# Attention and FFN in one kernel: the main heads begin beside the last early pairs, and fewer FFN pieces stand beside the first of them

## The chip, the cores and the metric

The kernel runs on one core of a Trainium2 chip. The core has five engines with an instruction queue each, and every queue is worked in order: TensorE (PE in the profile, its weight loads PEld), VectorE (DVE), ScalarE (ACT), GpSimd (POOL) and SyncE (SP), which here only issues DMAs. The metric is the device time of one execution in microseconds (us); lower is better.

## What is computed

Attention with a forget gate over 8 batches of 8 heads, 576 positions, head size 64, all in float32, and behind it a feed-forward network (FFN) over the 4608 rows of 512 that the attention leaves:

```
scores = scale * q @ k.T
cum    = cumsum(log(clip(f, 1e-4, 1)))
scores = where(causal, -1e9, scores + cum[:, None] - cum[None, :])
attn   = exp(scores - max); attn = attn / (sum + 1e-9)
x      = (attn @ v), heads side by side: 4608 x 512
h      = x @ w_in                 # 512 -> 2048
out    = max(0.01 * h, h) @ w_out # 2048 -> 512
```

## The kernel before

**Precision.** A float32 matmul is done as products of split numbers: each operand is a high part, rounded to the type float32r, and a low part (what the rounding left). Names that end in h and l (xh and xl, win_h and win_l, gh and gl, ph and pl) are such parts. For q and k the parts lie in the two halves of the 128 partitions: s1 and m1 hold high and low parts of one head's q and k, s2 and m2 (tiles fixed_s2a, fixed_m2b and so on, a and b by turns) the same crosswise, with the decay in spare rows.

**Two kinds of attention work.** The first 256 positions of three batches (NE = 3) are done ahead, two heads at a time, as 12 *early pairs* (functions early_load, early_scores, early_values; tiles qk, ve, ze, sce, tre, pte, ave, xe). This makes rows for the FFN soon, while its weights still come in: they are 16 pieces of a megabyte that load_weight fetches into two buffers (wraw) and splits on ACT and DVE. Then come the 64 *main heads*, t = 0 to 63, in the order of batches 0, 3 to 7, 1, 2. In batches 0, 1 and 2 a main head has 320 rows left (three row tiles, i = 2 to 4), in the others all 576 (five row tiles).

**A main head** passes through these steps. load(t) issues the DMAs of q and k into raw (one buffer) and of v into vm (one buffer). split(t) casts raw to s1 and m1 on ACT (L362, L363), copies parts of it to the other 64 partitions by DMA, and subtracts on POOL (minus, L149: m2 first, then s1) to get the low parts; v goes to fixed_vs, cast on ACT (L373), subtracted and shifted on POOL. scores(t, i) makes the row tile's scores on PE (sc), adds the mask and takes the row maximum on DVE (L395, into fixed_z0 to fixed_z4) and the exponential on ACT (L401); for the last tile POOL copies a corner of z4 (L407). In the next pass of the loop transposes(t, i) turns the tiles on PE (tr) and evacuates them on ACT (ph, L445) and DVE (pl, L447). values(t) multiplies with V (av) and adds the halves into x. After each second head, inverse and normalise make 1 / sum: its rows go by SP's queue to DRAM and come back spread over partitions (rows, rb and ph in the DMA lists).

**The FFN** takes 18 groups of 256 rows. It is a generator, ffn(), that yields after each *quantum*: 12 matmuls into h (half of a piece of 256 hidden units) or 6 into o (128 output rows). A piece p of a group is 4 quanta. Groups 0 and 1 are done in halves, pieces 0 to 3 of both and then 4 to 7 of both, since the weights come in that order; what the first halves leave is kept in the tiles part. The low part gl of the activation is made on POOL (L617) while heads run and on DVE else. Groups from 2 on are read back from DRAM (xs) and split by split_group: a cast on DVE (xh) and a subtraction of 128 x 1024 on POOL (xs, L149).

**What sets the order.** fill(n) adds n to a credit and takes as many whole quanta as it covers. Beside the early pairs the table FQ gives the credit of each step. In the loop over main heads a pass calls fill nine times' worth of step, and step is min(have / (left + SLACK), MAXQ) / 8: quanta at hand, divided by the passes left until new rows come, plus a reserve. The program so written is then listed for each engine by a scheduler, which may move instructions over one another where no dependence forbids it; tc.keep_in_program_order holds a single one in its place. So the order on each engine is that of the built program, not quite that of the text.

**Tiles that share buffers.** Tiles with one tag use the same buffer in turn. The fixed tiles of the main heads (fixed_z, vm, s2, m2, vs) are cleared once by fix(), on POOL. Before, the early pairs used the tags vm, s2b, m2b, s2a and m2a for half of their tiles (ZE and L316), so those fixed tiles could not be made until the pairs were done.

## Time and profile before

| | |
|---|---|
| median of three runs | 1210.83 us (1210.63, 1210.83, 1215.83) |
| the profiled execution | 1211.98 us, span 1210.2 |
| busy: PE, DVE, ACT, POOL | 98%, 52%, 53%, 38% |
| DMA | 110.55 MB, mean 91 GB/s |
| end of the early pairs (last ave), first score of head 0 | 145.5 us, 157.9 us |

The span is cut into 40 slices of 30 us on the page; each digit is the busy share of an engine in tenths, and PEclk the clock that the throttle granted to TensorE:

```profile
PE   9999989999999999999999999999999999999998
POOL 0000255555555444454444353534454544531000
PEclk9999999999999999999999999999999999999999
```

Matmuls are pipelined: one lasts longer in the trace than the distance to the next, so a PE that reads as busy all the time can still lose a little at every short wait.

### The profile page before, as it was taken

What the parts mean: (1) busy time and instruction counts of PE and PEld (TensorE: products, weight loads), DVE (VectorE), ACT (ScalarE), POOL (GpSimd) and SP (SyncE); (2) the same over time, 40 slices, a digit from 0 to 9 for tenths busy, and PEclk for the clock granted to TensorE, in tenths of its full rate; (3) what the DMA queues carried; (4) which work ended last, traced back from release to release, by engine and by line L of the source; (5) the groups of instructions that cost most, each with busy time, mean ns of one, the idle gap of its engine ahead of it and who ended that gap; (6) DMA issues with size and microseconds to landing.
All of it is one profiled execution on the core that took longest, in us unless ns stands there. A gap on an engine that the chain in (4) does not pass through costs nothing.

```text
span 1210.2 us, 22495 instructions
## 1 busy us (share of the span) xinstructions
PE 1190.7 (98%) x7812; PEld 1067.8 (88%) x7812; DVE 631.0 (52%) x1687; ACT 636.5 (53%) x1633; POOL 458.7 (38%) x471
## 2 busy tenths in 40 slices
PE   9999989999999999999999999999999999999998
PEld 6678879888899999899999999999999999999997
DVE  6898646566665555464544444445444444553221
ACT  6886456667665565555545445454445445651111
POOL 0000255555555444454444353534454544531000
PEclk9999999999999999999999999999999999999999
DMA  5555233344343233322332323232223223221000
GB/s 172 192 178 174 87 96 110 97 110 130 104 132 89 72 105 91 112 80 83 97 99 57 95 73 92 73 90 62 74 81 94 59 70 82 75 63 46 18 18 18
DMA packets 82129, 110.55 MB, mean 91 GB/s; under 512 B 20640, under 2 KB 51728, under 8 KB 82016
## 3 DMA queue, kind: packets, MB, share of 16 engines
q1 hardware_dynamic: 82016, 109.12, 31.1%
q8 instruction: 62, 1.02, 0.3%
q14 instruction: 51, 0.42, 0.1%
HBM read 65.32 MB, written 18.58 MB: 69 GB/s over the span
## 4 chain that ended last, share of the span: by engine, by line
PE 85%; DVE 4%; DMA 4%; ACT 3%; issue 2%; POOL 1%; SPq 0%; ACTq 0%; POOLq 0%; DVEq 0%
PE h L108 31%; PE o L108 29%; PE av L108 7%; PE tr L112 7%; PE sc L108 6%; PE sce L108 2%; PE warm L108 2%; PE ave L108 1%; DMA raw<-in_kT 1%; ACT fixed_z L401 1%; DMA wraw<-in_w_in 1%; DVE pl L447 1%; DVE fixed_z L395 1%; ACT ph L445 1%; PE tre L112 1%
## 5 line engine op out<-in xcount | busy, mean ns | idle before, releaser
L617 POOL TENSOR_TENSOR gl<-g,gh 128x512 fp32r<-128x512 f32 x111 | 145.4, 1310 | 249.1 <-DVE gh L615 246.4
L108 PE MATMUL o<-wout_h,gh 128*128 128x512 f32 x576 | 230.4, 400 | 0.0
L108 PE MATMUL o<-wout_l,gh 128*128 128x512 f32 x576 | 226.4, 393 | 0.0
L108 PE MATMUL o<-wout_h,gl 128*128 128x512 f32 x576 | 225.7, 393 | 0.0
L401 ACT ACTIVATE fixed_z<-fixed_z,max 128x192 f32<-128x192 f32 (+3 forms) x272 | 161.0, 592 | 98.8 <-DVE max L395 96.8
L108 PE MATMUL h<-xh,win_h 128*128 128x256 f32 x1152 | 208.0, 286 | 0.4 <-ACT xh L330 0.4
L612 ACT ACTIVATE g<-h 128x512 f32<-128x512 f32 x144 | 86.0, 597 | 222.0 <-PE h L108 213.2
L108 PE MATMUL h<-xh,win_l 128*128 128x256 f32 x1152 | 200.5, 283 | 0.4 <-DVE win_l L190 0.4
L445 ACT CAST ph<-tr 128x192 fp32r<-128x192 f32 (+3 forms) x360 | 126.4, 373 | 141.2 <-PE tr L112 96.0
L395 DVE CUSTOM_DVE_ANT_0 fixed_z<-sc,tri 128x192 f32<-128x192 f32 (+3 forms) x272 | 122.6, 453 | 149.5 <-PE sc L108 146.5
L615 DVE CAST gh<-g 128x512 fp32r<-128x512 f32 x144 | 77.7, 540 | 202.3 <-ACT g L612 200.6
L447 DVE TENSOR_TENSOR pl<-tr,ph 128x384 fp32r<-128x384 f32 (+3 forms) x296 | 137.7, 468 | 78.7 <-ACT ph L445 77.1
L108 PEld LDWEIGHTS h<-xh,win_h 128*128 128x128 f32 x1152 | 171.1, 190 | 6.1 <-ACT xh L330 0.9
L108 PEld LDWEIGHTS h<-xh,win_l 128*128 128x128 f32 x1152 | 165.0, 190 | 1.2 <-DVE win_l L190 0.6
L108 PE MATMUL h<-xs,win_h 128*128 128x256 f32 x1024 | 164.5, 283 | 0.0
L112 PE MATMUL tr<-ident_r,fixed_z 128*128 128x128 f32 x888 | 146.4, 275 | 9.1 <-POOL fixed_z L407 4.7
L108 PEld LDWEIGHTS h<-xs,win_h 128*128 128x128 f32 x1024 | 141.0, 192 | 0.0
L112 PEld LDWEIGHTS tr<-ident_r,fixed_z 128*128 128x128 f32 x888 | 107.5, 141 | 32.9 <-POOL fixed_z L407 5.6
L108 PEld LDWEIGHTS o<-wout_h,gl 128*128 128x128 f32 x576 | 108.2, 188 | 23.7 <-issue 0.2
L108 PEld LDWEIGHTS o<-wout_l,gh 128*128 128x128 f32 x576 | 108.8, 189 | 15.0 <-issue 0.2
L108 PEld LDWEIGHTS o<-wout_h,gh 128*128 128x128 f32 x576 | 108.6, 189 | 15.0
L108 PE MATMUL sc<-m,s 128*128 128x288 f32 (+1 forms) x336 | 120.6, 364 | 0.1
(111 smaller groups left out, 1687.1 us busy)
## 6 DMA issues: line engine op xcount, KB each, us to landing
raw<-in_kT SPq DMA_DIRECT2D x64, 144.0 KB
m<-m SPq DMA_DIRECT2D x64, 144.0 KB
wraw<-in_w_in SPq DMA_DIRECT2D x16, 512.0 KB
wraw<-in_w_out SPq DMA_DIRECT2D x16, 512.0 KB
fixed_vm<-in_v SPq DMA_DIRECT2D x64, 128.0 KB
xs<-xd SPq DMA_DIRECT2D x16, 512.0 KB
out<-ost SPq DMA_DIRECT2D x28, 256.0 KB
raw<-in_qT SPq DMA_DIRECT2D x40, 144.0 KB
```

Of the source, the lines that this page charges most:

```text
L108: nc.tensor.matmul(*args, **kw)
L112: nc.tensor.transpose(*args)
L395: nc.vector.tensor_tensor_reduce(out=z[:, a:b], in0=ps[:m, :b - a], in1=tri[:m, at:at + b - a], scale=-SCALE, scalar=3.0e38 if x == 0 else ...
L401: nc.scalar.activation(z, z, AF.Exp, bias=h["max"][:m, last:last + 1], scale=-1.0, accum_out=fixed["sum" + "ab"[s // 2 % 2]][:m, i, s % 2: ...
L445: nc.scalar.copy(strided(ph, run), source(ps, run))
L447: nc.vector.tensor_tensor(strided(pl, run), source(ps, run), strided(ph, run).bitcast(F32), op=ALU.subtract)
L612: nc.scalar.activation(g, ph, AF.Prelu, alpha=0.01)
L615: nc.vector.tensor_copy(gh, g)
L617: eng.tensor_tensor(gl, g, gh.bitcast(F32), op=ALU.subtract)
```

## The change

Heads 0 and 1 are loaded and split beside the early pairs: load(0) with v at pair 8 and load(1) at pair 11, split(0) at pair 10 and split(1) behind the last pair. For that, load and split are cut in two (load_v and split_v are the parts for v), fix() is called at the beginning and fix_z(), which clears z0 to z4 and takes the buffer of vs, in its old place. The early pairs get buffers of their own (tags e0 to e4), and so does the tile part of group 0 that lay in s1 (part1). FQ gives 10 quanta less beside the last two steps (4 and 2 for 8 and 8). In the loop over heads, CAPS bounds the first eight passes to 3 (times 9 / 8) quanta and the ninth to 5, and the reserve SLACK is 2 passes, not 3. Some of the moved DMAs and casts are held in program order. No instruction of the computation is added or left out.

```diff
--- before.py
+++ after.py
@@ -17,15 +17,16 @@
 DELAY = 90
 ORDER = (0, 3, 4, 5, 6, 7, 1, 2)
 HP = 4
-PARTS = (("part0", 1), ("s1", 2), ("ost", 2), ("ost", 2))
+PARTS = (("part0", 1), ("part1", 1), ("ost", 2), ("ost", 2))
 MAXQ = 9
-SLACK = 3
+CAPS = {**{t: 3 for t in range(8)}, 8: 5}
+SLACK = 2
 B2 = 5
 B4 = 4
 NE = 3
 WQ = (1, 1, 1, 1, 1, 1, 1, 1, 2, 2, 2, 2)
-ZE = (("z0", "z1", "z2", "z3"), ("vm", "s2b", "m2b", "s2a"))
-FQ = (0, 0, 0, 0, 4, 8, 8, 8, 8, 8, 8, 8, 8)
+ZE = (("z0", "z1", "z2", "z3"), ("e0", "e1", "e2", "e3"))
+FQ = (0, 0, 0, 0, 4, 8, 8, 8, 8, 8, 8, 4, 2)
 BUFS = dict(s1=2, m1=2, ost=2)
 RAWS = ("ph", "pl")
 WARM = (20, 4, 6)
@@ -243,14 +244,21 @@
         h = state[t] = {}
         a, n = c0 * P, S
         x = h["raw"] = one.tile([P, S], F32, tag="qraw", name=f"raw_{t}")
-        nc.sync.dma_start(x[:D, a:n], qT[s][:, a:n])
-        nc.sync.dma_start(x[D:, :n], kT[s][:, :n])
-        g, o = s // 2, s % 2
+        for y, src in ((x[:D, a:n], qT[s][:, a:n]), (x[D:, :n], kT[s][:, :n])):
+            last = nc.sync.dma_start(y, src)
+            if t < 2:
+                tc.keep_in_program_order(last)
+        if s % 2 == 0:
+            pairs[s // 2, c0] = {}
+
+    def load_v(t):
+
+        g, o = tasks[t][0] // 2, tasks[t][0] % 2
         vm = fixed["vm"]
-        nc.sync.dma_start(vm[:, :NFULL], v4[g][:, o])
-        nc.sync.dma_start(vm[:REST, NFULL], vr[g][:, o])
-        if o == 0:
-            pairs[g, c0] = {}
+        for y, src in ((vm[:, :NFULL], v4[g][:, o]), (vm[:REST, NFULL], vr[g][:, o])):
+            last = nc.sync.dma_start(y, src)
+            if t < 1:
+                tc.keep_in_program_order(last)
 
     early = {}
 
@@ -313,7 +321,7 @@
                 transpose(
                     ps[:, x * P:(x + 1) * P], e[c][:, j * P:(j + 1) * P], ident
                 )
-            pt = one.tile([P, 3 * P], F32, tag=("z4", "m2a")[o], name=f"pte_{b}_{g}_{o}")
+            pt = one.tile([P, 3 * P], F32, tag=("z4", "e4")[o], name=f"pte_{b}_{g}_{o}")
             nc.scalar.copy(pt, ps[:, :3 * P])
             pts.append(pt)
         out = psum.tile([P, 512], F32, tag="tr", name=f"ave_{b}_{g}")
@@ -335,18 +343,21 @@
     def fix():
 
         for x in "ab":
+            y = fixed["sum" + x] = one.tile([P, NCH, 2], F32, tag="sum" + x, name=f"fixed_sum{x}")
+            nc.gpsimd.memset(y, 1.0)
             for w, n in (("s2", 2), ("m2", 4)):
                 y = fixed[w + x] = one.tile([P, S], F32R, tag=w + x, name=f"fixed_{w}{x}")
                 nc.gpsimd.memset(y[:D].bitcast(F32), 0.0)
                 nc.gpsimd.memset(y[:n].bitcast(F32), 1.0)
-            y = fixed["sum" + x] = one.tile([P, NCH, 2], F32, tag="sum" + x, name=f"fixed_sum{x}")
-            nc.gpsimd.memset(y, 1.0)
+        vm = fixed["vm"] = one.tile([P, NCH, D], F32, tag="vm", name="fixed_vm")
+        nc.gpsimd.memset(vm[:, NFULL], 0.0)
+
+    def fix_z():
+
         for i in range(NCH):
             z = fixed[f"z{i}"] = one.tile([P, (i + 1) * P], F32, tag=f"z{i}", name=f"fixed_z{i}")
             nc.gpsimd.memset(z if i == 0 else z[:, i * P + REST:], 0.0)
-        vs = fixed["vs"] = one.tile([P, 2, NCH, 2 * D], F32R, tag="vs", name="fixed_vs")
-        vm = fixed["vm"] = one.tile([P, NCH, D], F32, tag="vm", name="fixed_vm")
-        nc.gpsimd.memset(vm[:, NFULL], 0.0)
+        fixed["vs"] = one.tile([P, 2, NCH, 2 * D], F32R, tag="vs", name="fixed_vs")
 
     def split(t):
 
@@ -359,8 +370,10 @@
         m1 = h["m1"] = one.tile([P, S], F32R, tag="m1", name=f"m1_{t}", bufs=2)
         s2, m2 = h["s2"], h["m2"] = fixed["s2" + x], fixed["m2" + x]
         raw = h["raw"]
-        nc.scalar.copy(s1[:D, a:n], raw[:D, a:n])
-        nc.scalar.copy(m1[D:, :n], raw[D:, :n])
+        for y, x in ((s1[:D, a:n], raw[:D, a:n]), (m1[D:, :n], raw[D:, :n])):
+            last = nc.scalar.copy(y, x)
+            if t < 2:
+                tc.keep_in_program_order(last)
         for y in (s1, s2):
             nc.sync.dma_start(y[D:, a:n].bitcast(F32), s1[:D, a:n].bitcast(F32))
         nc.sync.dma_start(m1[:D, :n].bitcast(F32), m1[D:, :n].bitcast(F32))
@@ -368,9 +381,13 @@
         nc.sync.dma_start(m2[:2, :n].bitcast(F32), dec_k[s][:, :n])
         minus(m2[D:, :n], raw[D:, :n], m1[D:, :n].bitcast(F32))
         minus(s1[:D, a:n], raw[:D, a:n], s1[:D, a:n].bitcast(F32))
-        o = s % 2
-        vs, vm = fixed["vs"][:, o], fixed["vm"]
-        nc.scalar.copy(vs[:, :, :D], vm)
+
+    def split_v(t):
+
+        vs, vm = fixed["vs"][:, tasks[t][0] % 2], fixed["vm"]
+        last = nc.scalar.copy(vs[:, :, :D], vm)
+        if t < 1:
+            tc.keep_in_program_order(last)
         minus(vs[:, :, D:], vm, vs[:, :, :D].bitcast(F32))
         nc.gpsimd.tensor_copy(vs[REST:, NFULL], vs[:REST, NFULL].bitcast(F32))
 
@@ -681,6 +698,7 @@
         compare_op=ALU.is_ge, fill=NEG,
     )
 
+    fix()
     steps = [(b, g) for b in range(NE) for g in range(HPB // 2)]
     early_load(0, 0)
     for n in range(len(RAWS)):
@@ -691,6 +709,12 @@
             early_load(*steps[x + 1])
         if x < len(steps):
             early_scores(b, g)
+            if x in (8, 11):
+                load(x // 11)
+            if x == 8:
+                load_v(0)
+            if x == 10:
+                split(0)
             weights(sum(WQ[:x + 1]))
         if x == 2:
             decay_rows()
@@ -698,19 +722,22 @@
             early_values(*steps[x - 1])
             if steps[x - 1][1] == HPB // 2 - 1:
                 ready[0] = (steps[x - 1][0] + 1) * T
+        if x == len(steps):
+            split(1)
         fill(FQ[x])
-    fix()
-    load(0)
-    split(0)
+    fix_z()
+    split_v(0)
     for t in range(nt + 1):
         heads[0] = t < nt
         if t + 1 < nt:
-            load(t + 1)
+            if t:
+                load(t + 1)
+            load_v(t + 1)
         before = list(range(max(tasks[t - 1][1] - 1, 0), NCH)) if t else []
         now = list(range(*tasks[t][1:])) if t < nt else []
         have = ready[0] // T * NQ - used[0]
         left = min((e + 2 - t for e in ends if e + 1 >= t), default=1)
-        step = min(have / (left + SLACK), MAXQ) / 8
+        step = min(have / (left + SLACK), CAPS.get(t, MAXQ)) / 8
         fill(step)
         for i in range(5):
             if i in before:
@@ -730,7 +757,9 @@
             if s % HPB == HPB - 1:
                 ready[0] = place[s // HPB, c0 * P] + S - c0 * P
         if t + 1 < nt:
-            split(t + 1)
+            if t:
+                split(t + 1)
+            split_v(t + 1)
         fill(step * (3 - len(spans(t - 1)) if t else 1))
     done.append(nt)
     for _ in range(NG * NQ):
```

What this moves on the engines, at three places. **PE, at the first scores of head 0** (sc_0_2 is its row tile 2; o_0_0_4 is FFN group 0, its second half, h_1_6 group 1's piece 6). Before:

```order
L108 MATMUL h_1_6_1756<-xh_1_155,win_l_6_112 128x256
L108 MATMUL h_1_6_1756<-xl_1_156,win_h_6_104 128x256
L108 MATMUL sc_0_2_0_1770<-m1_0_1736,s1_0_1735 128x320
L108 MATMUL sc_0_2_0_1770<-fixed_m2a_1704,fixed_s2a_1701 128x320
L108 MATMUL sc_0_3_0_1775<-m1_0_1736,s1_0_1735 128x448
```

Now:

```order
L109 MATMUL o_0_0_4_1449<-wout_l_6_128,gh_0_6_1567 128x512
L109 MATMUL o_0_0_4_1449<-wout_h_6_120,gl_0_6_1568 128x512
L109 MATMUL sc_0_2_0_1668<-m1_0_1319,s1_0_1318 128x320
L109 MATMUL sc_0_2_0_1668<-fixed_m2a_167,fixed_s2a_164 128x320
L109 MATMUL sc_0_3_0_1673<-m1_0_1319,s1_0_1318 128x448
```

The scores stood behind 55 quanta, into the last quarter of group 1; they now stand behind 45, in group 0's piece 6.

**POOL, at the split of group 2** (fixed_z4 is the copy that finishes a head's last tile; the number behind raw, m1 and s1 is the head that is prepared). Before, from head 0's copy to head 1's:

```order
L407 COPY fixed_z4_1725<-fixed_z4_1725 64x64
L149 TENSOR_TENSOR fixed_m2a_1704<-raw_2_1828,m1_2_1936 64x576
L149 TENSOR_TENSOR s1_2_1935<-raw_2_1828,s1_2_1935 64x320
L149 TENSOR_TENSOR fixed_m2b_1712<-raw_3_1955,m1_3_2074 64x576
L149 TENSOR_TENSOR xs_2_1754<-xs_2_1754,xh_2_1901 128x1024
L407 COPY fixed_z4_1725<-fixed_z4_1725 64x64
```

Now, from head 4's copy to head 5's:

```order
L424 COPY fixed_z4_1653<-fixed_z4_1653 64x64
L150 TENSOR_TENSOR fixed_vs_1655<-fixed_vm_178,fixed_vs_1655 128x5x64
L392 CAST fixed_vs_1655<-fixed_vs_1655 64x128
L150 TENSOR_TENSOR xs_2_2002<-xs_2_2002,xh_2_2182 128x1024
L150 TENSOR_TENSOR fixed_m2a_167<-raw_6_2220,m1_6_2300 64x576
L634 TENSOR_TENSOR gl_1_7_2217<-g_1_7_2214,gh_1_7_2216 128x512
L150 TENSOR_TENSOR s1_6_2299<-raw_6_2220,s1_6_2299 64x320
L150 TENSOR_TENSOR fixed_m2b_175<-raw_7_2326,m1_7_2442 64x576
L424 COPY fixed_z4_1653<-fixed_z4_1653 64x64
```

The split moved from the second head to the sixth, with four more pieces of POOL work between the same two copies; in both lists a whole load (raw_3, raw_7) lies between them.

**ACT, from head 1's last exponential** (ph_1 is the evacuation of head 1's transposes). Before:

```order
L362 CAST s1_3_2073<-raw_3_1955 64x320
L363 CAST m1_3_2074<-raw_3_1955 64x576
L401 ACTIVATE fixed_z4_1725,fixed_suma_1707<-fixed_z4_1725,max_1_1854 128x576
L506 COPY x_0_1904<-av_0_0_1905 64x320
L373 CAST fixed_vs_1727<-fixed_vm_1728 128x5x64
L612 ACTIVATE g_1_7_1929<-h_1_7_1871 128x512
L445 CAST ph_1_1960<-tr_1_1_1962 128x64 x2
```

Now:

```order
L418 ACTIVATE fixed_z4_1653,fixed_suma_162<-fixed_z4_1653,max_1_1730 128x576
L523 COPY x_0_1782<-av_0_0_1783 64x320
L388 CAST fixed_vs_1655<-fixed_vm_178 128x5x64
L374 CAST s1_3_1937<-raw_3_1825 64x320
L374 CAST m1_3_1938<-raw_3_1825 64x576
L462 CAST ph_1_1830<-tr_1_1_1832 128x64 x2
```

The casts that wait for head 3's load went behind the exponential, directly ahead of the evacuation.

## The prediction

> **What bounds the kernel now.** I read the page first (busy shares, the clock line), then TensorE (PE) in stretches of time, then the chain of waits where a stretch is not full, and last the queues that the chain names.
>
> ```profile
> span 1210.2 us, 22495 instructions
> PE 1190.7 (98%) x7812; PEld 1067.8 (88%) x7812; DVE 631.0 (52%) x1687; ACT 636.5 (53%) x1633; POOL 458.7 (38%) x471
> ```
>
> The PE is the bound: 98% of the span, the others near half. The change adds and removes no PE work, so it can win only PE time that is lost today. Where that is, the PE by stretches shows (stretch, its length, PE busy and matmuls, clock, DMA share, GB/s; below it, matmuls into the accumulators o alone):
>
> ```profile
> 157.90:182.70 24.80, 21.71 (x135) 0.93 0.28 74
> 182.70:221.40 38.70, 38.70 (x261) 1.00 0.37 103
> 229.90:335.20 105.30, 99.04 (x663) 1.00 0.41 112
> 335.20:380.00 44.80, 44.80 (x309) 1.00 0.41 120
> 640.10:697.50 57.40, 57.40 (x387) 1.00 0.30 82
> ```
>
> ```profile
> 182.70:221.40 38.70, 12.68 (x48) 1.00 0.37 103
> 229.90:335.20 105.30, 28.83 (x108) 1.00 0.41 112
> 640.10:697.50 57.40, 23.27 (x91) 1.00 0.30 82
> ```
>
> ```profile
> 1133.68 2.75 PE o L108 x12
> 1198.24 2.87 PE h L108 x24
> ```
>
> 157.9 is the first score of head 0; 182.7 to 221.4 are four heads of 320 rows, from one product with V to the next, 229.9 to 335.2 nine heads, nearly all of 576 rows, 640.1 to 697.5 three. A quantum is 12 h or 6 o matmuls; from the last stretch of the chain (nothing but FFN) it costs (2.75 + 2.87) / 4 = 1.405 us. Three o matmuls go with one quantum, so the stretches hold 16, 36 and 30 quanta. A short head's own PE time is then (38.70 - 16 x 1.405) / 4 = 4.06 us, a full head's (57.40 - 30 x 1.405) / 3 = 5.08.
>
> So two places lose time. **Loss A**, the start of the heads: 24.80 - 21.71 = 3.09 us idle, and a clock of 0.93, which costs 0.07 x 24.8 = 1.7: 4.8 us. **Loss B**, the first full heads: 36 x 1.405 + 9 x 5.08 = 96.3 of 105.3 us, so 9.0 lost (6.3 shown as idle, the rest hides in the latency of pipelined matmuls). They have 4 quanta each; right behind, with 6 to 8 quanta, no idle time is left.
>
> What ends the wait in A, from the chain (start, us, what):
>
> ```profile
> 160.10 2.19 DMA raw<-in_qT
> 162.39 0.47 ACT s L362
> 163.41 2.12 DMA fixed_s2a<-s
> 165.89 0.88 POOL s L149
> 166.79 0.49 SPq L246
> 167.33 2.75 DMA raw<-in_kT
> 170.94 1.43 POOL fixed_m2b L149
> 172.45 2.36 POOL xs L149
> 174.89 0.30 POOL fixed_z L407
> ```
>
> This is the load path of a head: load q and k, cast on ScalarE (ACT), copy to the other 64 partitions, subtract on GpSimd (POOL), and only then the next load, since raw has one buffer. One round is 166.79 - 160.10 = 6.7 us. At 172.45 the split of FFN group 2 (xs) stands on POOL ahead of the copy that finishes head 1's last tile, and the transposes wait. The clock follows:
>
> ```profile
> 175.00:180.00 5.00, 4.77 (x20) 0.67 0.27 76
> 235.59 0.44 PE L112 MATMUL tr<-ident_r,fixed_z 128*128 128x128 f32 x2 [1.60 <-POOL fixed_z L407]
> 235.00:240.00 5.00, 4.33 (x25) 1.00 0.27 65
> PE tr L112 <- POOL fixed_z L407: 4.7, 3, 2.1
> ```
>
> After the longest such wait, 2.1 us, the clock is 0.67 for 5 us, 1.65 us more; after one of 1.6 us it stays 1.00.
>
> **The change part by part.** *Head 0 begins earlier.* Its first score stands behind 55 quanta in the old list of the PE and behind 45 in the new one. The 10 quanta between are PE work without a gap, 1.405 us each: it can begin 14 us earlier, at 157.9 - 14 = 144. Its inputs would be there: the memsets that filled POOL from 143.5 now stand at its beginning, where POOL idled:
>
> ```profile
> 126.94 0.69 POOL L346 MEMSET fixed_z<- 128x128 f32 x4 [124.93 <-PE tre L112]
> 138.19 1.22 DVE L190 TENSOR_TENSOR wout_l<-wraw 128x1024 fp32r<-128x1024 f32 x1
> ```
>
> Four loads (raw and vm of head 0) pass ahead of six weight pieces on SyncE's (SP's) queue, and raw of head 1 stands between the halves of the last one. At 0.5 us an issue the weights come 2 to 3 us later, the last at 139.4 + 3 = 142.4. The first product with it now stands behind most of head 1's scores, past 148, so this costs nothing; without that cover it would cost up to 3 us. The new tags (part1, e0 to e4) take waits away and cost SBUF only. Loss A goes, all but what the new start waits itself: **-4.8**.
>
> *Full heads.* From the first product with V of head 8 to that of head 15 the PE's list now holds 38.8 quanta, not 28; by head 15 both have spent 118. That is 5 to 6 a head, a period of 5.08 + 5.5 x 1.405 = 12.8 us instead of 11.7. I keep 1.6 of loss B for the heads with 5 and for the step from short to full heads: **-7.4** (bounds: 9.0, all of it, and 3, should the load path below and not the filling set two thirds of it).
>
> *Short heads.* 20.5 quanta stand between the products of heads 0 and 6, 3.4 a head: 4.06 + 3.4 x 1.405 = 8.8 us instead of 9.7. The load path must keep up. SP's queue shows when the loads start:
>
> ```profile
> 189.39 0.49 SPq L246 DMA_DIRECT2D raw<-in_qT  x1
> 197.45 0.50 SPq L246 DMA_DIRECT2D raw<-in_qT  x1
> 207.90 0.55 SPq L246 DMA_DIRECT2D raw<-in_qT  x1
> 216.68 0.54 SPq L246 DMA_DIRECT2D raw<-in_qT  x1
> 228.89 0.49 SPq L246 DMA_DIRECT2D raw<-in_qT  x1
> 233.15 0.67 ACT L363 CAST m<-raw 64x576 fp32r<-64x576 f32 x1 [0.78 <-DMA raw<-in_kT]
> ```
>
> The rounds take 8.1, 10.4, 8.8 and 12.2 us, 9.9 in the mean: longer than 8.8, though they partly waited for the PE themselves. ACT works in order, so a late load holds what stands behind its cast (last row). The new order puts the casts of head 3 ahead of the evacuation of head 1's transposes. Worked there: k lands 0.55 + 2.75 us after the issue, its cast takes 0.67, the evacuation and the subtraction some 1.1, so the next transposes can start 5.1 us after the issue; the PE comes 3.7 us after it, since the issue waits for POOL's subtraction of head 2. That is 1.4 us of wait. The same sum gives 0.3 to 0.6 at heads 0, 3 and 4. **+2.6**; bounds 0 (round of 6.7) and 6 x (9.9 - 8.8) = 6.6.
>
> *The split of group 2.* It now falls into head 5, and POOL must do one load more before it copies head 5's tile z4. Durations beside those above:
>
> ```profile
> L617 POOL TENSOR_TENSOR gl<-g,gh 128x512 fp32r<-128x512 f32 x111 | 145.4, 1310 | 249.1 <-DVE gh L615 246.4
> 195.43 0.87 POOL L149 TENSOR_TENSOR fixed_vs<-fixed_vm,fixed_vs 128x320 fp32r<-128x320 f32 x1
> 199.59 1.43 PE h L108 x12
> 201.03 0.44 PE tr L112 x4
> 201.46 0.52 PE sc L108 x4
> 202.22 1.46 PE av L108 x9
> 204.89 1.39 PE o L108 x6
> ```
>
> From the end of head 3's product with V: 0.9 us on ACT (copy and cast of V), then on POOL vs 0.9 and its shift, taken as 0.5, xs 2.4, m2 1.4, gl 1.3, s 0.9: 8.3. Then the load that waited for s: 0.55 + 2.75, cast 0.7, m2 1.4, copy 0.3: 14.0 us. The PE has meanwhile, by its new list, 5 quanta (7.0), head 4's product (1.46), 12 transposes at 0.11 and 8 score matmuls at 0.13 (2.4), and the 0.3 of wait counted above: 11.2. It waits 2.8. That is over 2.1, so I add the 1.65 of a slow clock: **+4.4**; bounds 0 (the split fits into POOL's idle time) and 6 (xs starts a further 1.6 us later).
>
> The Trainium skill, "TensorE: Matmul & The Clock Gate" (section "HAM oscillation — how this bites in real kernels"), says that only idle gaps above about 3.4 us throttle the clock. By that rule the new wait would cost no slow clock, and the time would be 1.65 us lower. The rows above (2.1 us of idle time, then 0.67) speak against it, so the sum keeps the 1.65.
>
> *The rest.* The end is FFN alone in both, 77 quanta after the last product before and 72 now; nothing is lost there today, so nothing changes.
>
> Sum: -4.8 - 7.4 + 2.6 + 4.4 = **-5.2 us**. The profiled execution took 1211.98 us, 1.8 of it around the span: 1206.8. It lies 1.15 above the median of the three runs, 1210.83, so on that scale I predict **1205.6**.
>
> **The rivals.**
> 1. *All waits are covered.* The split falls into POOL's idle half and the loads run ahead. For it: the round can be 6.7 us, and POOL is busy 38%. Against it: z4 of head 5 stands behind another head's load. -4.8 - 9.0 + 1 = -12.8: **1198.0**.
> 2. *The load path becomes the pace of the short heads*, at 9.9 us. For it: the four rounds above. Against it: some of them waited for the PE. Six heads lose 6.6 instead of 2.6, and the full heads keep 2 more: -5.2 + 4.0 + 2.0 = +0.8: **1211.6**.
> 3. *Slower: the clock falls at each late load.* One wait over 2 us costs its 2.1 and 1.65 of slow clock, 3.75. If five of the short heads have such a wait, 18.8 us stand against 12.2 of gain, with the split's 4.4: +11: **1221.8**. It decides from four heads on (15.0 + 4.4 - 12.2 = +7.2; three make +3.5, within half a per cent). Against it: head 1's wait by my sum is 1.4, and 1.6 left the clock at 1.00.
> 4. *The order changes and the time does not*: head 0 stands 10.7 quanta earlier but its data are late. It would need a delay of over 10 us past 125, where the casts stand now; the PE would idle, and A returns: **1210**.
>
> **How the numbers follow.** Forecast 0.48, rivals 0.14, 0.28, 0.06 and 0.04. The forecast's own range is 1202 to 1209. The range must leave out at most 2 in 10: from **1198.5** to **1212.5** it leaves out rival 3, half of rival 1 and a little of rival 2. Half a per cent, what a measurement of this kernel can tell from no change, is 6.05 us: below 1204.8 is faster, above 1216.9 slower. Of the forecast 0.45 lies below 1204.8, which makes 0.22; with rival 1 and a little of rival 2, **0.37 faster**; **0.56 within**; **0.07 slower**.
>
> **What would show it.** Right: head 0's first score near 144 and no wait of 2 us around it; idle time of the PE of at most 2 us over the nine heads that take 105.3 us today; one wait of 2 to 4 us ended by POOL's z4 copy, with xs just ahead of it on POOL, and a clock under 0.9 behind it. Wrong: several such waits among the first eight heads (rivals 2 and 3), or none (rival 1); full heads that still wait with 5 and 6 quanta, which would mean that the load path and not the filling sets loss B; a first head later than 150.

## The result, and the profile after

| | before | after |
|---|---|---|
| median (7 runs each) | 1210.91 us | 1217.94 us |
| ratio to before, 95% interval | | 1.0050 (1.0034 to 1.0065) |
| profiled execution, its span | 1211.98, 1210.2 | 1217.53, 1215.8 |

The changed kernel is 0.5% slower, about 6 us; the forecast was 5 us faster. The head of its page (span; busy time and share of each engine, with the number of instructions):

```profile
span 1215.8 us, 22473 instructions
PE 1193.4 (98%) x7812; PEld 1068.4 (88%) x7812; DVE 619.4 (51%) x1684; ACT 637.1 (52%) x1633; POOL 463.9 (38%) x474
```

PE is as full as before, so a share says nothing here. The stretches of the changed kernel do (stretch, length, busy time and instructions of PE, PEld, DVE, ACT and POOL, clock, DMA share, GB/s). They begin 1.6 us ahead of the first score of head 0 and are cut at the first product with V of heads 1, 6, 15, 16, 18 and 63; from head 15 to 16 and from 18 to 63 none is shown:

```profile
143.00:165.20 22.20, 19.93 (x133) 17.56 (x133) 12.62 (x42) 14.07 (x38) 11.62 (x15) 1.00 0.46 129
165.20:215.50 50.30, 46.19 (x299) 41.16 (x298) 32.36 (x87) 31.49 (x82) 28.94 (x31) 0.97 0.38 105
215.50:331.90 116.40, 115.27 (x779) 104.75 (x778) 66.02 (x209) 75.16 (x206) 57.20 (x58) 1.00 0.37 102
346.80:384.60 37.80, 34.86 (x223) 31.57 (x222) 16.66 (x50) 18.48 (x50) 16.52 (x16) 0.95 0.32 92
1107.50:1212.10 104.60, 103.44 (x647) 92.72 (x645) 22.51 (x42) 14.10 (x24) 4.76 (x2) 1.00 0.07 23
```

The full heads (third row) lose 1.1 us of idle time in 116.4; the kernel before lost 6.3 in 105.3. That worked. But the short heads idle for 4.1 us at a clock of 0.97, the stretch around head 17 for 2.9 at 0.95, and the end, where FFN runs alone, for 1.2. In the kernel before, PE was busy for all but 0.02 us of the last two stretches, from head 16 to 18 and in the end:

```profile
348.70:380.00 31.30, 31.30 (x212) 28.70 (x211) 19.56 (x49) 18.34 (x50) 16.61 (x15) 1.00 0.38 110
1097.20:1206.60 109.40, 109.38 (x694) 99.23 (x693) 25.71 (x44) 14.72 (x25) 4.79 (x2) 1.00 0.07 22
```

To see what a stage costs beyond its work, two kernels are compared at the same product with V: the difference of the start times, plus 1.405 us for every quantum that the first kernel's PE list has less ahead of it. At head 6: 215.5 - 229.9 us and 13.25 quanta fewer, so -14.4 + 18.6 = +4.2 us late. The table gives the lag against the profiled execution of before that each stage adds. "Start" ends at head 1, "short" at 6, "full" at 16, "17" at 18, "middle" at 63, "end" at the last matmul. Times of runs on different chips are compared by their ratios, which are to runs of before on the same chip. The names are: E the early start, C the caps, R the reserve of 2; numbers in brackets are the 95% interval in units of 0.0001 above or below 1.

| kernel | start | short | full | 17 | middle | end | sum | median us | ratio |
|---|---|---|---|---|---|---|---|---|---|
| after = E+C+R | -1.8 | +6.0 | -7.5 | +5.1 | +1.5 | +2.2 | +5.5 | 1217.94 | 1.0050 (+34, +65) |
| e1 E+C | -2.0 | +7.2 | -7.5 | +0.7 | +2.5 | +0.6 | +1.5 | 1213.63 | 1.0018 (+4, +32) |
| e2 R | -3.1 | +1.0 | -1.2 | +2.5 | +0.2 | +1.7 | +1.1 | 1211.41 | 1.0005 (-5, +16) |
| e3 C | -4.0 | +7.2 | -2.1 | -0.2 | -0.4 | 0.0 | +0.6 | 1213.04 | 1.0016 (+5, +27) |
| e4 E | -1.2 | +0.8 | -3.0 | +0.3 | +1.0 | +0.6 | -1.5 | 1208.89 | 0.9980 (-30, -9) |
| e10 E+R | -3.6 | +1.4 | +3.6 | +1.4 | +2.8 | +2.2 | +7.7 | 1217.89 | 1.0051 (+35, +66) |
| e6 E+C, R behind head 16 | -1.9 | +5.7 | -7.9 | +1.2 | +1.7 | +2.2 | +1.0 | 1214.37 | 1.0025 (+14, +35) |
| e5 after, last 8 heads 4 | -2.0 | +7.1 | -7.5 | +5.2 | +4.8 | +0.7 | +8.3 | 1220.24 | 1.0069 (+51, +87) |
| f2 after, near split early | -1.1 | +6.9 | -7.5 | +1.1 | +1.7 | +2.2 | +3.3 | 1215.18 | 1.0026 (+15, +36) |
| f5 E+R, near split early | -3.8 | +1.4 | -0.9 | 0.0 | +2.9 | +2.2 | +1.8 | 1214.72 | 1.0044 (+30, +57) |
| e7 E+C, xs of group 2 on DVE | -2.1 | +6.1 | -7.5 | +0.7 | +2.4 | +0.6 | +0.2 | 1212.63 | 1.0013 (+2, +25) |
| e8 E+C, group 2 split in head 2 | -2.3 | +6.4 | -7.1 | +0.7 | +2.5 | +0.6 | +0.8 | 1212.56 | 1.0003 (-11, +17) |
| e9 E+C, two raw (tag x) | +1.7 | +2.6 | -7.5 | +0.7 | +2.7 | +0.6 | +0.8 | 1213.12 | 1.0009 (-1, +20) |
| f1 E+C, two raw | -2.1 | +4.1 | -7.5 | +0.7 | +2.7 | +0.6 | -1.5 | 1211.08 | 0.9995 (-17, +7) |
| f3 after, two raw, near split early | 0.0 | +4.1 | -7.5 | +1.0 | +1.9 | +3.0 | +2.6 | 1214.32 | 1.0018 (+7, +29) |
| f4 E, two raw | -3.7 | +0.8 | -3.1 | +0.2 | +1.6 | +0.6 | -3.5 | 1209.46 | 0.9979 (-33, -9) |
| f6 E, two raw, caps on heads 5 to 8 | -2.5 | +2.1 | -4.7 | +1.4 | +2.2 | +0.6 | -0.9 | 1211.10 | 1.0002 (-10, +14) |
| e12 before, two raw | -2.0 | 0.0 | +1.5 | 0.0 | -0.1 | 0.0 | -0.6 | 1211.71 | 0.9995 (-14, +4) |
| e11 before, room taken | -1.7 | 0.0 | -0.2 | 0.0 | -0.1 | 0.0 | -2.0 | 1210.60 | 0.9987 (-24, -3) |

The last row is a measure of what not to read: e11 issues the order of before, and still stands 0.13% off. Stages are one execution each; ratios closer than some 0.15% are not told apart. Two things say how far a stage may be read. After, e1, e5, e6 and f2 have the same order on every engine as far as head 6's product, and their short stages scatter from +5.7 to +7.2. And some executions hold a stretch of half clock (last section), which takes 1.7 us: before in its start, so that every other kernel looks better there; after and e5 to e8 in the short stage; e2, e12 and (twice as long) e10 in the full one; after, e5 and e10 in 17.

**Where the time went: two places.** The longest waits of the changed kernel (engine and line, for whom; total us, times, longest), line numbers now those of the changed file:

```profile
PE tr L113 <- DVE ph L469: 6.7, 5, 3.1
PE h L109 <- POOL xs L150: 3.5, 2, 2.4
```

The first, behind head 3's product at head 4's transposes, in the timeline (start, us, engine, line, out<-in, count, idle time and what ended it; SP, ACT, POOL, DVE and PE rows in turn):

```profile
182.85 0.50 SPq L248 DMA_DIRECT2D raw<-in_qT  x1
183.45 1.18 SPq L547 DMA_DIRECT2D rb<-rows  x2
184.74 1.17 SPq L547 DMA_DIRECT2D ph<-rows  x2
185.97 0.59 SPq L248 DMA_DIRECT2D raw<-in_kT  x1
...
189.03 0.67 ACT L374 CAST m<-raw 64x576 fp32r<-64x576 f32 x1 [1.67 <-DMA raw<-in_kT]
189.72 0.60 ACT L629 ACTIVATE g<-h 128x512 f32<-128x512 f32 x1
190.21 0.55 ACT L462 CAST ph<-tr 128x64 fp32r<-128x64 f32 x3
...
189.36 2.34 POOL L150 TENSOR_TENSOR xs<-xs,xh 128x1024 fp32r<-128x1024 f32 x1
...
190.35 1.64 DVE L632 CAST gh<-g 128x512 fp32r<-128x512 f32 x1 [0.99 <-ACT g L629]
192.27 0.23 DVE L469 TENSOR_TENSOR ph<-tr,ph 64x64 fp32r<-64x64 f32 x1
...
192.65 0.52 PE L113 MATMUL tr<-ident_r,fixed_z 128*128 128x128 f32 x3 [3.09 <-DVE ph L469]
```

The four reads of the normaliser (rb and ph, 2.4 us of issue) stand between the q and the k of one load, head 6's. ACT waits 1.67 us for k, and behind its cast stand g and the evacuation for which PE waits. The late k is not the whole of the 3.1 us: g's cast on DVE (gh) then falls beside POOL's subtraction and takes 1.64 us instead of a usual 0.43, ahead of DVE's part of the evacuation.

The second is the split of group 4, seen in the same way (SP, DVE, POOL, PE):

```profile
340.48 0.51 SPq L583 DMA_DIRECT2D xs<-xd  x1
...
349.48 0.68 DVE L588 CAST xh<-xs 128x1024 fp32r<-128x1024 f32 x1
...
349.57 1.87 POOL L150 TENSOR_TENSOR s<-raw,s 64x576 fp32r<-64x576 f32 x1 [0.78 <-DVE x L524]
351.40 2.33 POOL L150 TENSOR_TENSOR xs<-xs,xh 128x1024 fp32r<-128x1024 f32 x1
...
353.79 0.74 PE L109 MATMUL h<-xs,win_h 128*128 128x256 f32 x4 [2.36 <-POOL xs L150]
```

FFN stands at group 4 and its low part isn't there. The end has the same wait, at group 16, in the chain of waits of the changed kernel:

```profile
1116.56 0.61 DVE xh L588
1117.17 0.07 issue
1117.24 2.37 POOL xs L150
1119.61 0.04 issue
1119.66 2.17 PE h L109 x16
```

### The profile page after: what moved, and what is told of

Same layout as the page of the kernel before. It is cut to its first block, busy times and chain, and to the rows that moved or that the text cites. A ratio compares the mean times of both kernels' runs of the same rounds, so it can differ in the third digit from the quotient of the medians.

```text
span 1215.8 us, 22473 instructions
## 1 busy us (share of the span) xinstructions
PE 1193.4 (98%) x7812; PEld 1068.4 (88%) x7812; DVE 619.4 (51%) x1684; ACT 637.1 (52%) x1633; POOL 463.9 (38%) x474
## 4 chain that ended last, share of the span: by engine, by line
PE 89%; DMA 3%; ACT 3%; DVE 2%; issue 1%; POOL 1%; SPq 1%; ACTq 0%; POOLq 0%; DVEq 0%
PE h L109 31%; PE o L109 30%; PE tr L113 8%; PE av L109 7%; PE sc L109 7%; PE sce L109 2%; DMA wraw<-in_w_in 2%; PE warm L109 2%; PE ave L109 1%; DMA raw<-in_kT 1%; POOL xs L150 1%; ACT wt L177 0%; PE tre L113 0%; ACT ph L462 0%; ACT g L629 0%
## 5 line engine op out<-in xcount | busy, mean ns | idle before, releaser
L634 POOL TENSOR_TENSOR gl<-g,gh 128x512 fp32r<-128x512 f32 x114 | 149.3, 1309 | 271.4 <-DVE gh L632 269.6
L632 DVE CAST gh<-g 128x512 fp32r<-128x512 f32 x144 | 71.3, 495 | 195.0 <-ACT g L629 193.5
```

The lines of the kernel that those rows point to most:

```text
L632: nc.vector.tensor_copy(gh, g)
L634: eng.tensor_tensor(gl, g, gh.bitcast(F32), op=ALU.subtract)
```

## The experiments

### The three parts, alone and together

Theory A: the smaller reserve costs the time. Rival B: the early start and the short heads do. e1 is the changed kernel, e2 and e3 are the kernel before with one part:

```diff
 e1, E+C, on after:  -SLACK = 2          +SLACK = 3
 e2, R, on before:   -SLACK = 3          +SLACK = 2
 e3, C, on before:   +CAPS = {**{t: 3 for t in range(8)}, 8: 5}     -MAXQ)   +CAPS.get(t, MAXQ))
 e4, E, on after:    -CAPS = {...}       +CAPS = {}      -SLACK = 2   +SLACK = 3
 e10, E+R, on after: -CAPS = {...}       +CAPS = {}
```

> Theory A (the smaller reserve is what costs): the changed kernel with 3 steps in reserve again. FFN then reaches group 4 with 5 quanta after head 16's first product with V (1.2 in the changed kernel, 2.0 before) and group 16 with 499 quanta behind it at head 63 instead of 504, so both waits for xs (3.5 and 1.3 us with their slow clock: 5.1 and 2.2 us) go, and the time falls by 6 to 7 us, to 1211 (heads 8 to 15 get 36 quanta, not 38.8: up to 1 us back). Rival B (the early start and the load path of the short heads cost it, the waits for xs only show where time lost elsewhere comes out): 1216 to 1218, with PE idle elsewhere.

> The kernel before with 2 steps in reserve and nothing else. Theory A: group 4 is reached 1.3 quanta after head 16's product and head 63 has 504 quanta behind it, as in the changed kernel: waits for xs of 2 to 3 us at group 4 and of 1 to 2 us at group 16, 5 to 7 us more than before: 1216 to 1218. Rival B: within 1.5 us of before, 1210 to 1212.

> The kernel before with at most 3 quanta in the first 8 heads and 5 in the ninth, reserve 3, no early start. Heads 8 to 15 get 29.8 quanta instead of 28, so only about 2 of the 9 us lost there return; the short heads get 2.6 quanta each instead of 2.9 where the load path is already the limit at the start. Theory A: 1208 to 1211. Rival B (short heads with 3 quanta are limited by the load path): 1213 to 1216.

> The early start alone: the changed kernel without the caps and with 3 steps in reserve. Theory A: the start of the heads gains its 2 to 3 us (4.8 less some 1.5 to 2 for weights that come later), the full heads lose their 9 as before, no wait for xs at groups 4 and 16: 1207 to 1210. Rival B (the early start costs as much as it gains): 1211 to 1215.

> The changed kernel without the caps: early start and 2 steps in reserve. FFN reaches group 4 already between heads 15 and 16. Theory A (a smaller reserve costs its waits for xs wherever FFN is ahead, and the early start puts it ahead): 4 to 5 us over the early start alone (1208.9), 1212.5 to 1214. Rival B (as in the kernel before, where the smaller reserve cost 0.3 us net, what the waits take the full heads' larger filling gives back): 1208.5 to 1210.

Measured ratios: 1.0018, 1.0005, 1.0016, 0.9980, 1.0051. Neither theory held alone. Putting the reserve back takes 0.32% off the changed kernel (4 us of 6; A expected 6 to 7), and the two xs waits go (17: +5.1 to +0.7, end: +2.2 to +0.6). But the caps cost too: E+C stands 0.38% above E. The early start alone is the only part that gains, and its 0.20% is little more than the 0.13% of e11, which changes no order.

e2 missed A's time and showed its waits: 3.2 us for xs at groups 3 and 4 and 1.2 at group 16. The heads ahead of group 3, better filled, had gained about as much in its profile: its lag at head 8 is -4.7 us, of which 1.7 is the half clock of before. With the early start and without caps (e10) the same reserve costs 0.71%: its wait for xs at group 3 is longer (2.3 us, 1.9 in e2), and a slow clock follows it (waits of e10 from 245 to 360 us, and its stretch behind the longest):

```profile
PE h L109 <- POOL xs L150: 3.5, 2, 2.3
```

```profile
263.00:268.00 5.00, 5.00 (x23) 4.81 (x23) 2.48 (x7) 2.62 (x6) 0.00 (x0) 0.50 0.21 59
```

From head 8 to 9 the lag grows by 6.0 us there, 3.4 of them the clock of this one execution; in e4 it grows by 0.0. With 3 in reserve the caps cost 0.38%; with 2 they cost nothing (E+R 1.0051, E+C+R 1.0050), presumably since they hold back the quanta that the reserve no longer does; no run isolates that.

### Where the reserve costs

```diff
 e5, after:       -(left + SLACK)   +(left + SLACK + 2 * (t >= nt - 8))
 e6, after:       -(left + SLACK)   +(left + SLACK + (t < 17))
 f2, after; f5, e10:
     -work[0] >= since[n] + DELAY // (1 + near[0])
     +work[0] >= since[n] + (15 if near[0] else DELAY)
```

> The changed kernel with 2 more steps in reserve over the last 8 heads alone (497.7 quanta behind it at head 63 instead of 504). Theory A: the wait for xs of group 16 (1.3 us, 2.2 with what follows) goes, the one of group 4 stays: 1215 to 1216.5. Rival B (the wait only shows where time lost elsewhere comes out): 1217 to 1218.

> The changed kernel with 3 steps in reserve up to head 16 and 2 behind it: group 4 is reached 4 quanta after head 16's first product with V (1.2 in the changed kernel), the end is as in the changed kernel. Theory A: the wait of 2.5 us for xs of group 4 and its slow clock go, 3 to 4 us less (5.1, less 1 for the full heads' fewer quanta): 1214 to 1215; the wait at group 16 stays. Rival B: 1217 to 1218.

> The changed kernel with nothing but an earlier split where FFN is near: 15 matmuls after the fetch instead of 45, so that the split of group 4 stands 9 instructions earlier on VectorE. Theory A (the rows of group 4 are there at about 344; what PE waits for is a split that stands late in the lists of VectorE and GpSimd): the wait of 2.5 us at 351 falls to 0 to 1, 1213 to 1215; the wait at group 16, where the rows themselves come late, stays. Rival B (the rows are late): 1217 to 1218.

> Early start and 2 steps in reserve without the caps (1217.9, 8.6 us over the early start with 3 steps in reserve), with the split 15 matmuls after the fetch where FFN is near; groups 3 and 4 are then split 5 and 3 instructions earlier on VectorE. Theory A (late splits): the waits of 2.4 us at group 3 and 1.4 us at group 4 fall under 1, 1213 to 1215. Rival B (without the caps FFN stands at groups 3 and 4 before their rows are there): the wait at group 3 stays over 1.5 us, 1216 to 1218.

e6 came as A expected: group 4's wait falls to 0.3 us and the ratio from 1.0050 to 1.0025. f2 reaches the same, 1.0026, with the full amount of FFN ahead: only the split stands earlier (rows of f2, DVE and POOL):

```profile
347.39 0.69 DVE L588 CAST xh<-xs 128x1024 fp32r<-128x1024 f32 x1 [1.51 <-DMA xs<-xd]
...
348.17 2.50 POOL L150 TENSOR_TENSOR xs<-xs,xh 128x1024 fp32r<-128x1024 f32 x1 [6.46 <-DVE xh L588]
```

Now DVE waits for the rows, and PE has no wait for xs near group 4. In f2 they landed 5.3 us after their fetch (342.09, on SP). Fetched at 340.48 in the changed kernel, they were there at some 345.8 by that, while the split stood 3.7 us further down, at 349.48. So PE waited for a split late in the lists, not for late rows. f5 says the same of groups 3 and 4 without caps by its trace (no wait for xs from 245 to 360 us, full: +3.6 to -0.9, 3.4 of this from e10's half clock), but waits for DVE's row maximum have grown from 0.7 to 2.3 us, and its ratio, 1.0044 against e10's 1.0051, doesn't show the gain in time; medians alone differ by 3.2 us. That stays unclear.

e5 missed: it took the end's wait away (+2.2 to +0.7) and came out slower, since FFN held back is taken from the last heads: the products of heads 54 to 58 stand 4 to 5 quanta apart, not 5 to 7, and a wait of 2.1 us for POOL's z4 copy opens at 1044.7 us, between those of heads 57 and 58. As far as head 55 both kernels lose the same 1.9 us in the middle; the whole difference (+1.5 to +4.8) lies behind it. In the end a reserve and a full PE draw on the same quanta.

### What the short heads wait for

Theory A of this set is first the split of group 2, then the load path. All stand on e1, f4 on e4 and e12 on before (fc, an early tile that shares the tag qraw, gets bufs=2 with it):

```diff
 e7:  -minus(xs, xs.bitcast(F32), xh.bitcast(F32))
      +eng = nc.vector if n == 2 else nc.gpsimd
      +eng.tensor_tensor(xs, xs.bitcast(F32), xh.bitcast(F32), op=ALU.subtract)
 e8:  -since[n] + DELAY // (1 + near[0])   +since[n] + (50 if n == 2 else DELAY // (1 + near[0]))
 e9, f1, f4, e12:
      -tag="qraw", name=f"raw_{t}")   +tag="qraw", name=f"raw_{t}", bufs=2)
 e9:  -tag=("z4", "e4")[o]            +tag=("z4", "x")[o]
 f1, f4:  -("part1", 1)               +("m1", 2)
```

> On the base of the run with 3 steps in reserve (1213.6): the subtraction that makes xs of group 2 is done by VectorE instead of GpSimd. Theory A (the 3.3 us wait at head 3 and the 2.2 us wait at head 4 come from GpSimd's 2.3 us subtraction: VectorE is held beside it, and the tail of GpSimd's queue is late): only the 1.5 us that ACT waits for k at head 3 stay, heads 0 to 5 lose 3 to 4 us less: 1209.5 to 1211. Rival B (the load path alone is too slow for 3 quanta a head, whoever splits): 1213 to 1214, with waits of the same size for DVE ph and POOL z.

> On the same base (1213.6): group 2 is split 50 matmuls after its fetch instead of 90, so that its two instructions stand in head 2, behind that head's load and not beside an odd head's normalisation; GpSimd still does it. Theory A (what costs is the place: beside the late k of head 6 and VectorE's evacuation): 1210 to 1212. Rival B (the split costs the same in any short head): 1213 to 1214.

> On the base with 3 steps in reserve (1213.6): raw, the tile that takes a head's q and k, gets two buffers, so that a load no longer waits for GpSimd's subtractions of the head before (for the room, the second transposed early tile goes to the tag x). Theory A (what the caps cost in the short heads is the load path: k behind the normaliser's four transfers on SP's queue and behind GpSimd): no wait of 2 us or more at heads 3 and 4, heads 0 to 5 lose 1 to 2 us instead of 6.8: 1207 to 1209.5. Rival B (the order of ACT and DVE, or the split, sets the 3 us wait): it stays at 2.5 to 3.3 us, 1212 to 1214.

> The early start and the caps with 3 steps in reserve (1213.6) and two buffers for raw, as in the run with raw doubled, but the room now comes from part1, which goes to the tag m1; the early tiles keep their own tags. Theory A (the load path is what the caps cost in the short heads; in the run before, the early tile on the tag x gave it back with a 4.1 us wait for pte): the early part loses 1 to 2 us as without raw doubled, heads 0 to 5 lose 3 us or more less than the 6.8 us: 1208 to 1210. Rival B (the loads that come earlier disturb the early part by themselves): the wait for pte stays at 3 to 4 us, 1212 to 1213.

> The early start alone (1208.9) with raw doubled (room from part1). Theory A (the load path limits the heads with about 4 quanta too): 1 to 2 us less, 1206.5 to 1208. Rival B (with 4 quanta the load path is covered, as the kernel before with raw doubled suggests, 0.5 us): 1208.5 to 1209.5.

> The kernel before with two buffers for raw and nothing else. Theory A (the load path limits the heads wherever they have 4 quanta or fewer): the 4.8 us lost at the start of the heads fall to 2 to 3, the 9.0 us lost in the first full heads to 6 or less: 1206 to 1208.5. Rival B (the filling sets the full heads' loss, as the prediction had it, and the start waits for the split on GpSimd): 1210 to 1211.

With POOL's subtraction on DVE (e7) the wait at head 4's transposes stayed, at 2.9 us (a row of the waits, and ACT's wait for k):

```profile
PE tr L113 <- DVE ph L469: 5.3, 5, 2.9
```

```profile
188.27 0.67 ACT L374 CAST m<-raw 64x576 fp32r<-64x576 f32 x1 [1.38 <-DMA raw<-in_kT]
```

Split in head 2 (e8), it was 2.5 us. The short stages, +6.1 and +6.4, lie within the scatter of the unchanged order (+5.7 to +7.2), so neither run shows a worth of the split, let alone the 3 to 4 us that A expected. Nor does either set DVE free: in e7 it makes the subtraction itself (1.30 us) and ends its normalisation only at 191.25 us; ACT's evacuation starts behind that, 1.84 us after ACT was done with g; in e8 gh takes 1.10 us beside POOL's subtraction of m2. With two buffers for raw (f1) k goes out ahead of the normaliser's reads, and ACT waits for it no more (SP and ACT rows, then the waits from 165 to 216 us):

```profile
181.46 0.54 SPq L248 DMA_DIRECT2D raw<-in_qT  x1
182.61 0.47 SPq L248 DMA_DIRECT2D raw<-in_kT  x1
183.82 1.09 SPq L547 DMA_DIRECT2D rb<-rows  x2
...
185.08 0.67 ACT L374 CAST m<-raw 64x576 fp32r<-64x576 f32 x1
```

```profile
PE tr L113 <- DVE ph L469: 1.7, 2, 1.0
PE tr L113 <- POOL fixed_z L424: 1.0, 1, 1.0
```

The short stage falls to +4.1 (f3: +4.1 too, e9: +2.6), clear of the scatter, and the ratio from 1.0018 to 0.9995. So the load path is the one part of the short heads' loss that these runs show, some 2 to 4 us of it; the 2.6 to 4.1 that are left weren't traced to one cause. e9 gave the gain back in its early part, by its own tag: a wait for pte of 4.1 us. Without caps the load path is covered: f4 against e4, and e12 against before, show no difference (rival B of each).

### Both repairs, late caps, and the place of tiles

f3 is the changed kernel with f1's and f2's edits; f6 is f4 with CAPS = {5: 3, 6: 3, 7: 3, 8: 5}; e11 only takes the room of the new tags:

```diff
 e11, before:
+    for tag, w in (("part1", 4 * P), ("e0", P), ("e1", 2 * P), ("e2", P), ("e3", 2 * P), ("e4", 3 * P)):
+        nc.gpsimd.memset(one.tile([P, w], F32, tag=tag, name=f"pad_{tag}")[:, :1], 0.0)
```

> The changed kernel, caps and 2 steps in reserve included, with both: raw doubled (room from part1) and the split 15 matmuls after the fetch. If the load path and the late split of group 4 are the two causes of the loss, and they add up: 1217.9 less 4 to 5 and less 3 to 4, 1209 to 1211. If one theory falls, its part stays: 1213 to 1215.

> A version built from the parts: early start, raw doubled, 3 steps in reserve, caps of 3 for heads 5 to 7 and 5 for head 8 alone, so that the first heads keep their 4 quanta and heads 8 to 15 get 30.7 instead of 29.5. Theory A (the caps pay where they feed the full heads and cost where the load path is short): 0.5 to 1.5 us under the same kernel without caps, 1207.5 to 1209. Rival B (3 quanta cost in any short head what they bring later): 1209 to 1211.

> The kernel before, with the room of the new tags (part1, e0 to e4) taken and not used: only where the other tiles lie changes, and six GpSimd memsets of one column stand at the start. It tests the slow drift: in the runs with the new tags the spacing of matmuls into o is 232 ns in the median and of those into sc 173 to 175 over heads 18 to 56, against 231 and 172 without, and they lose 1 to 2.5 us between heads 18 and 63. Theory A (the place of the tiles does it): 231 becomes 232, the end comes 1 to 2 us later, 1212 to 1213. Rival B (it follows from the order): 231 and 172 as before, 1211.

f3, 1.0018, is 0.32% under the changed kernel and not the 0.6% expected: both repairs work in their stages (17: +1.0; the short stage +4.1), but the start gives 1.8 us less and the end 0.8 more, in one execution of it. f6 missed: 1.0002, no better than without caps; its full heads gain 1.6 us more than f4's, and every other stage but the end loses. No version beat the early start alone: e4 and f4, 0.2% under before, which is near what these ratios can tell. In e11 the matmuls into o keep their 231 ns, so the room of the new tags doesn't make the drift of 1 to 3 us that all kernels with the early start show in the middle (232 ns; for e5 as far as head 55). What does, stays open.

## Why the prediction was wrong

**The step that failed** is "The rest. The end is FFN alone in both ... nothing is lost there today, so nothing changes". It was put at 0 and measured +8.8 us: 5.1 at group 4 (2.4 of wait and 1.7 of half clock behind it among them), 1.5 in the middle, 2.2 at group 16. The middle is the drift whose cause is open; the two other places are where FFN meets rows that must be split first. That nothing is lost there today was right; that so nothing changes was not, since the kernel before was only just in time there. e1, e6 and f2 take the 17 stage back to between +0.7 and +1.2, and e1 the end to +0.6. The profile of before had the number. From the last head's product to the end of POOL's split of group 16 (PE and POOL rows of before):

```profile
1097.15 0.75 PE L108 MATMUL av<-ph,fixed_vs 128*128 128x320 f32 x5
...
1106.18 2.39 POOL L149 TENSOR_TENSOR xs<-xs,xh 128x1024 fp32r<-128x1024 f32 x1 [12.18 <-DVE xh L571]
```

That is 11.4 us. Its PE list had 11 quanta of group 15 left there, 15.5 us, 1.5 for the product itself and 1.0 for eight matmuls that need only xh: 18.0. The new one has 6 quanta: 8.4 + 1.5 + 1.0 = 10.9, less than 11.4. The wait came out at 1.2, as the path took 12.1 (1107.52 to 1119.61). Of the reserve I had asked what it brings to the full heads, not what it had covered.

**Start, -4.8.** Measured -1.8. The first score came as forecast, near 144 (PE row of the changed kernel):

```profile
144.57 0.31 PE L109 MATMUL sc<-m,s 128*128 128x320 f32 x1
```

But the term was mis-sized twice. Loss A did not go: PE still idles 2.3 us of the 22.2 (first stretch), 1.7 of them in one wait for DVE's ph at head 1's transposes, against 3.1 of 24.8 before. And e11, with the order of before, is 1.7 us faster in the same stage: the slow clock that I counted as 1.7 of the loss belongs to one execution (below). Against e11 the new start gains 0.1 us; what e4 gains stands in its full heads (-3.0). At head 0's first product the changed kernel is even 0.3 us behind before, though it idled only 0.5 us ahead of it and before 1.0: ACT now waits 4.1 us for weights between 100 and 145 us, 1.2 before. "So this costs nothing" is doubtful then; no run isolated it.

**Short heads, +2.6 for the load path and +4.4 for the split.** Together +7.0 forecast, +6.0 measured (5.7 to 7.2 in the five executions of this order), the size by luck of two errors. The price was put on the wrong cause: no worth of the split shows beyond the scatter (e7, e8), while two buffers for raw take 2 to 4 us away (f1, f3, e9). The wait stood at head 4's transposes, not at head 5's, and hung on a late k and on gh beside POOL's subtraction, not on POOL's z4 copy. The forecast wait for that copy came in two executions of this order, e1 (2.1 us) and f2 (1.8), but in e1 POOL had idled 5.3 us shortly before it, for ACT's cast of the next load's k: not the split either. The sum had k 0.6 us behind q on SP's queue; four other transfers came between. It is nearest to rival 2's mechanism (the load path as the pace), without its 2 us in the full heads.

**Full heads, -7.4.** Measured -7.5. The filling sets this loss, as the forecast had it; e12 shows that the load path doesn't (full: +1.5 with raw doubled, 1.7 of it half clock). The caps and the early start together bring it; C alone brings 2.1, E alone 3.0.

**The slow clock.** The prediction took 1.65 us of it after any wait over 2.1 us. The size is right where it comes (1.7), but not that it always comes; see the last section.

**Sum.** -1.8 + 6.0 - 7.5 + 8.8 = +5.5, the difference of the two profiled executions (1217.53 - 1211.98). None of the rivals had the reserve in it; the slower one asked for slow clocks in five short heads, and only one wait of over 2 us came there.

## What to carry to other kernels

A reserve is read by what it covers: for every change that lets a consumer run ahead, list the places where it meets its producer, and compare the work left there with the producer's path, even where no time is lost today. Where two small changes draw on the same work (here FFN quanta to fill with, and FFN quanta to hold back), run each alone and both together before either is trusted. A load that is issued in two halves is as late as its later half: look at what the queue puts between them.

## What the runs showed of the hardware that was not expected

Whether a wait of 2.1 to 3.3 us slows PE's clock differs from one execution of an order to the next. Of 24 gaps of over 1.6 us in the twenty profiles (from 150 to 1120 us, each counted beyond the usual distance of two matmuls), the seven under 2.0 us and six of the seventeen over it were followed by a clock of 1.00; eleven by one of 0.50 to 0.77 in the next 3 us, worth some 1.4 to 3.1 us each. What decides, the clock records of the traces show. In every execution the granted clock changes only on a grid of 3.41 us, whose place differs from execution to execution, and a half clock (0.50) lasts one cell of it, in e10 once two. Of the cells at full clock between 150 and 1120 us, all nine with 1.94 us or more of idle PE were followed by half clock, three of the six with 1.76 to 1.92 us, and none with less. So a wait counts by how much of it falls into one cell, and the same wait in the same order went both ways. The kernel before, at 175 to 180 us, had 0.67 after a wait of 2.1 us; e11, the same order, a wait of 2.3 us and 1.00 (its waits from 165 to 200 us, and its stretch):

```profile
PE tr L114 <- POOL fixed_z L409: 2.3, 1, 2.3
```

```profile
175.00:180.00 5.00, 4.87 (x34) 4.48 (x35) 2.29 (x8) 2.70 (x9) 3.35 (x5) 1.00 0.27 76
```

The two cells of the grid around that wait (length, PE busy and matmuls, clock, DMA share, GB/s), of before and then of e11: PE idles 1.9 us of the first cell in before, 1.8 in e11.

```profile
173.29:176.71 3.42, 1.48 (x8) 1.00 0.00 0
176.71:180.12 3.41, 3.41 (x15) 0.50 0.40 112
```

```profile
173.35:176.77 3.42, 1.64 (x8) 1.00 0.02 5
176.77:180.18 3.41, 3.41 (x29) 1.00 0.40 112
```

The wait of 3.1 us behind head 3's product in the changed kernel was followed by 0.76, that of 3.2 us in e1 by 1.00 (the stretch from 195 to 200 us of the changed kernel, then of e1):

```profile
195.00:200.00 5.00, 5.00 (x31) 4.73 (x30) 1.50 (x5) 2.30 (x5) 0.87 (x2) 0.76 0.23 63
```

```profile
195.00:200.00 5.00, 5.00 (x39) 4.69 (x37) 1.50 (x5) 1.38 (x3) 0.20 (x1) 1.00 0.21 56
```

The Trainium skill, "TensorE: Matmul & The Clock Gate" (section "HAM oscillation — how this bites in real kernels"), gives the rule "no PE-idle gaps >~3.4µs"; here eleven gaps of 2.1 to 3.3 us were followed by a lower clock, and six weren't. A slow clock seen once behind such a wait is neither a price nor a loss to win back.

A cast on DVE (gh, 128x512) took 1.64 us beside POOL's subtraction of xs at 189.36 us in the changed kernel; the median of its 144 is 0.43 us. The twenty traces tell whose work holds it. All 312 casts into gh that took over 0.6 us began while an operation of POOL ran, and ended 0.28 to 0.29 us after POOL's operation did (here 191.70 and 191.99); and no cast that began with more than 0.43 us of a POOL operation left was shorter. So the late load cost twice here: the operations behind it started later, and beside a subtraction of POOL.
